# Where a fused attention and MLP kernel computes the products of its packs: beside the gates, or beside the projection

## The chip, the core and the metric

The kernel runs on one core of one Trainium2 chip. TensorE (PE) multiplies matrices into PSUM, VectorE (DVE), ScalarE (ACT) and GpSimd (POOL) do the rest, and SyncE (SP) issues the transfers. The metric is the device time of one execution, in microseconds (us). Before the change it is 1799.77 us, the median of 3 runs (1798.51 to 1803.16).

## The reference

Three stages follow each other. First an attention in which 32 packed queries per head stand between the sequence and itself, for 8 batches x 8 heads, 576 positions, 64 wide. Then a gated MLP (512 to 1536 to 512) with a root-mean-square norm, and a second MLP (512 to 2048 to 512) on 4608 tokens:

```
p_packed = softmax_attention(p, k, v)             # 32 rows per head
x        = softmax_attention(q, p_packed, p_packed)
xn = x / sqrt(mean(x*x) + 1e-6) * rms_g
g, val = xn @ w_gate, xn @ w_val
x  = (g * sigmoid(g) * val) @ w_out
h  = x @ w_in2
out = (h * sigmoid(1.702 * h)) @ w_out2
```

The weights arrive as 64-bit floats.

## The kernel before

**Two numbers for one.** Operands are fp32 values split into a high part (a cast to a reduced fp32) and a low part (the remainder), and each product is three matmuls: high x high, high x low, low x high. So most results in PSUM are read twice: ACT casts the high part, and DVE or POOL subtracts it to get the low part.

**Units, steps and pairs.** The eight batches go in four units of two batches (`o` = 0, 1). The first MLP's 1536 hidden features go in 12 steps of 128, so there are 48 steps `s`, numbered through the units. Two steps (`G = 2`) make a pair, and there are 24 pairs.

**The products of the packs.** The attention's second half is linear in `p_packed`, so the kernel never forms `x` for the gate. Per step it multiplies the packed rows (`L`, scaled by `rms_g`) with the step's columns of `w_gate` and `w_val`, and has a small matrix per head group: these are the packs' products, `prods(s)`, line 604. One call is two groups of six matmuls into a PSUM bank `ps_w` (L622), and each group is read by two ACT casts to `Wh` (L624) and two DVE subtractions to `Wl` (L625), for 64 partitions each. `Wh` and `Wl` have two buffers each.

**The gate phase.** `gateval(s, o)`, line 640, multiplies the attention weights `Aqh`, `Aql` of batch `o` with `Wh`, `Wl`: four banks `ps_g` of six matmuls (L653). ACT takes the tanh (L660), DVE makes two passes (L661, L663), which also free the banks, and when the step's `th` is complete ACT casts it to `Hh` (L668) and POOL subtracts to `Hl` (L669).

**The projection.** After both steps of a pair, `close` calls `project` for both batches and four blocks `m` of 128 output features: two banks `ps_o` of six matmuls (L684) each. A bank is added to the accumulator by DVE (L694), or copied by ACT to `add` (L698) and added by POOL (L700); in the first pair of a unit it is copied by ACT (L691).

**One pool of banks.** `ps_w`, `ps_g` and `ps_o` rotate through the same five PSUM banks (`mm`, `MMB = 5`).

**The order.** `run` is a generator: it yields the estimated ns of PE's work after each piece, and the caller puts other work in between: the attention of the next unit (its rows in the trace are `ps_at`), in unit 0 the conversion of the first MLP's weights, in unit 3 that of the second MLP's. A conversion (`convert`, line 98) is an ACT pass, four DVE passes (L106 to L109), an ACT cast (L110) and a POOL subtraction (L111). A scheduler then orders each engine's instructions by a simulated timeline, with the program's order as priority, so what stands next to what on an engine is its choice within the dependencies. Each engine runs its list in order.

**Where the products stood.** `both(s, o, ahead)` runs a gate phase and takes a group from `ahead` after its first and its fourth bank:

```
for n, ns in enumerate(gateval(s, o)):
    yield ns
    if ahead is not None and n in (0, 3):
        yield next(ahead, 0)
```

In step `s` the call for `o` = 0 gets `prods(s + 1)` (line 747). So both steps of a pair carry a product in their first half, and the projection carries none.

**The loads.** Converted weights lie in DRAM for units 1 to 3. `load_wg` (three buffers of 1 MB) and `load_wo` (two buffers of 0.5 MB) fetch them through SP's queue.

After the 48 steps the second MLP (L854, L873) runs from about 1000 us to the end; the change doesn't touch it.

Of the kernel before, what the change touches and what calls it, by code (L numbers as in the profile page):

```python
# [22 lines left out]
def fl(t):  # L23

    return t.bitcast(F32)
# [3 lines left out]
def tile_pack_attention__then__two_mlps(  # L29
# [34 lines left out]
    NF1 = F1 // P  # L64
    NF2 = F2 // P
    NM = DM // P
    G = 2
# [7 lines left out]
    WGB = 3  # L75
# [447 lines left out]
    def mlp1(cv, lp, mm, getL, getAT):  # L523
        steps = [(u, j) for u in range(NU) for j in range(NF1)]
        wo, wg, Wp, hh, Aq = {}, {}, {}, {}, {}
# [64 lines left out]
        def have(d, s):  # L590
            while s not in d:
                assert piece()

        def load_wg(s):
            if NF1 <= s < len(steps):
                wg[s] = new("wg", s)
                nc.sync.dma_start(fl(wg[s]), wg_d[steps[s][1]])

        def load_wo(s):
            if NF1 <= s:  # L600
                wo[s] = new("wo", s)
                nc.sync.dma_start(fl(wo[s]), wo_d[steps[s][1]])
# [70 lines left out]
        def project(ss, o, m):  # L673
            u, j0 = steps[ss[0]]
            b = 2 * u + o
            for e in range(2):
                cols = slice(e * HS, (e + 1) * HS)
                ps = mm.tile([P, 512], F32, tag="mm", name="ps_o")[:, :HS]
                n = 0
                for s in ss:  # L680
                    oh, ol = wo[s][:, 0], wo[s][:, 1]
                    Hh, Hl = hh[s, o]
                    for st, mv in ((oh, Hh), (oh, Hl), (ol, Hh)):
                        nc.tensor.matmul(  # L684
                            ps, st[:, m * P : (m + 1) * P], mv[:, cols], start=n == 0, stop=n == 3 * len(ss) - 1
                        )
                        n += 1
                if j0 == 0:
                    if e == 0:
                        acc[o, m] = main.tile([P, S], F32, tag=f"acc{o}{m}", name=f"acc{o}{m}", bufs=1)  # L690
                    nc.scalar.copy(acc[o, m][:, cols], ps)  # L691
                elif m == 1 or m % 2 and u:
                    a = acc[o, m][:, cols]
                    nc.vector.tensor_add(a, a, ps)  # L694
                else:
                    if e == 0:
                        t = main.tile([P, S], F32, tag="add", name="add", bufs=2)
                    nc.scalar.copy(t[:, cols], ps)  # L698
                    if e == 1:
                        nc.gpsimd.tensor_add(acc[o, m], acc[o, m], t)  # L700
                if e == 0:
                    yield 365 * G
            if j0 + len(ss) == NF1:
                nc.sync.dma_start(x2_d[b][:, m], acc[o, m])
            yield 365 * G

        def run():
            nonlocal main
            main = pools["main"]

            def close(ss):
                for s in ss:
                    have(wo, s)
                for o in range(2):
                    for m in range(NM):
                        yield from project(ss, o, m)
                for t in ss:
                    Wp.pop(t)
                    wo.pop(t)
                    used["wo"] = t + 1  # L720
                    for o in range(2):
                        hh.pop((t, o))

            def both(s, o, ahead=None):
# [4 lines that stand above are left out]
                if ahead is not None:  # L729
                    next(ahead, None)  # L730


            yield from prods(0)
            scaled(0, 0)
            yield from both(0, 0, prods(1))
            yield from both(1, 0)
            yield "attention"
            scaled(0, 1)
            yield "next"
            yield from both(0, 1)  # L740
            yield from both(1, 1, prods(2))
            yield from close([0, 1])
            for s, (u, j) in enumerate(steps):
                if s < G:
                    continue
                load_wo(s)
                yield from both(s, 0, prods(s + 1))
                load_wg(s + WGB)
                yield from both(s, 1)
                if j == NF1 - 1:  # L750
                    yield "attention"
                    scaled(u + 1, 0)
                    scaled(u + 1, 1)
                if j % G == G - 1:
                    yield from close(list(range(s - G + 1, s + 1)))
                if j == NF1 - 1:
                    yield "unit"

        return fetch, piece, run
# [152 lines left out]
    with ExitStack():  # L912
# [8 lines left out]
        with ExitStack() as st1:  # L921
# [56 lines left out]
            u, ahead = 0, None  # L978
            every = EVERY / len(todo)
            spent, done = 0.0, 0.0  # L980
            for what in run():
# [7 lines left out]
                elif what == "unit":  # L989
# [4 lines left out]
                    elif u + 1 == NU:  # L994
# [3 lines left out]
                        ahead = early()  # L998
# [60 lines left out]
```

## Time and profile before

| | |
|---|---|
| median of 3 runs | 1799.77 us |
| the profiled execution | 1803.39 us, span 1801.6 us |
| granted TensorE clock, mean | 0.985 |
| PE busy | 1714.9 us (95%), 9976 matmuls |
| DVE busy | 969.9 us (54%) |
| ACT busy | 697.0 us (39%) |
| POOL busy | 511.7 us (28%) |
| matmuls of the products, L622 | 576, from 63.6 to 977.0 us |
| matmuls of the gates, L653 | 2304, from 72.1 to 986.5 us |
| matmuls of the projection, L684 | 2304, from 112.1 to 999.2 us |

Units can be told by the transfers of finished accumulators: unit 0 ends near 363 us, unit 2 near 807 us, unit 3 near 1000 us. The page's shares are means over these stages and the second MLP, so a table of stretches is read beside it. In such a table a line gives the bounds of a stretch in us from the span's start, its length, then per engine the busy us and the number of instructions in brackets, the granted clock (1.00 is 2.4 GHz, and a stretch that lies wholly at 1.2 GHz would show 0.50), the share of the DMA engines' time and GB/s. In a list of waits a line says who waited for which instruction, for how long in total, how often, and the longest.

### The profile page before, as it was taken

How to read it: one execution, taken by the hardware profiler on the slowest of the kernel's cores; microseconds unless marked ns; L12 is line 12 of the kernel's file. 1: busy time of each engine (PE TensorE's matmuls, PEld its weight loads, DVE VectorE, ACT ScalarE, POOL GpSimd, SP SyncE). 2: the span in 40 equal slices, each digit the busy share in tenths (PEclk: the TensorE clock that was granted, in tenths of full speed). 3: DMA queues.
4: the chain of work that ended last, by engine and by line, in shares of the span. 5: the costliest groups of instructions: out<-in, count | busy, mean ns of one | idle time of the engine just before them, and what ended most of it. 6: DMA issues, size and time to landing. Idle time of an engine off the chain costs nothing.

```text
span 1801.6 us, 26222 instructions
## 1 busy us (share of the span) xinstructions
PE 1714.9 (95%) x9976; PEld 1520.3 (84%) x9976; DVE 969.9 (54%) x1971; ACT 697.0 (39%) x1644; POOL 511.7 (28%) x470
## 2 busy tenths in 40 slices
PE   7798888999999999988899999999999999999998
PEld 5587877999999999978799788888888888888887
DVE  6979999856656666688955482122222222222221
ACT  5665655665555655556544331111111111111111
POOL 2546665644554345444544230000000000000000
PEclk9989998999999999999999999999999999999999
DMA  9654445454434542268731731010101010000000
GB/s 239 187 175 148 130 142 201 148 162 134 132 115 135 161 124 94 71 205 280 261 130 43 263 94 47 1 47 1 47 1 47 1 47 17 31 1 24 1 24 24
DMA packets 154462, 186.26 MB, mean 103 GB/s; under 512 B 87648, under 2 KB 124512, under 8 KB 147296
## 3 DMA queue, kind: packets, MB, share of 16 engines
q1 hardware_dynamic: 154336, 184.58, 32.0%
q8 instruction: 79, 1.29, 0.3%
q14 instruction: 47, 0.39, 0.1%
HBM read 139.46 MB, written 45.09 MB: 102 GB/s over the span
## 4 chain that ended last, share of the span: by engine, by line
PE 78%; DVE 16%; issue 2%; DMA 2%; ACT 2%; SPq 1%; POOL 0%; ACTq 0%; DVEq 0%; POOLq 0%
PE ps_dn L873 22%; PE ps_up L854 22%; PE ps_o L684 13%; PE ps_g L653 12%; DVE w L108 3%; PE ps_w L622 3%; DVE w L109 2%; PE ps_at L264 2%; DVE Wl L625 2%; DVE w L107 2%; DVE w L106 2%; PE ps_at L253 2%; DVE th L663 1%; PE ps_at L309 1%; DVE th L661 1%
## 5 line engine op out<-in xcount | busy, mean ns | idle before, releaser
L854 PE MATMUL ps_up<-xh,wi 128*128 128x512 f32 x1152 | 381.7, 393 | 2.3 <-DMA wi<-w 1.6
L873 PE MATMUL ps_dn<-wo,gh 128*128 128x512 f32 x1152 | 356.6, 391 | 0.0
L684 PE MATMUL ps_o<-Hh,wo 128*128 128x288 f32 x1536 | 332.1, 302 | 19.3 <-DVE th L661 9.0
L860 DVE CAST gh<-gf 128x512 fp32r<-128x512 f32 x144 | 62.4, 433 | 508.1 <-ACT gf L857 508.0
L857 ACT ACTIVATE gf<-ps_up 128x512 f32<-128x512 f32 x144 | 85.9, 597 | 610.3 <-PE ps_up L854 589.6
L684 PEld LDWEIGHTS ps_o<-Hh,wo 128*128 128x128 f32 x1536 | 255.5, 191 | 24.8 <-DVE th L661 9.9
L653 PE MATMUL ps_g<-Aqh,Wh 128*128 128x288 f32 x768 | 238.9, 312 | 23.5 <-ACT Wh L624 10.0
L854 PEld LDWEIGHTS ps_up<-xh,wi 128*128 128x128 f32 x1152 | 216.2, 188 | 52.0 <-POOL wo L111 2.0
L873 PEld LDWEIGHTS ps_dn<-wo,gh 128*128 128x128 f32 x1152 | 216.3, 188 | 47.5
L653 PE MATMUL ps_g<-Aql,Wh 128*128 128x288 f32 x768 | 229.5, 299 | 0.0
L684 PE MATMUL ps_o<-Hl,wo 128*128 128x288 f32 x768 | 228.2, 299 | 0.0
L653 PE MATMUL ps_g<-Aqh,Wl 128*128 128x288 f32 x768 | 228.1, 299 | 0.0
L854 PE MATMUL ps_up<-xl,wi 128*128 128x512 f32 x576 | 225.8, 392 | 0.0
L873 PE MATMUL ps_dn<-wo,gl 128*128 128x512 f32 x576 | 224.6, 391 | 0.0
L669 POOL TENSOR_TENSOR Hl<-th,Hh 128x576 fp32r<-128x576 f32 x96 | 141.0, 1469 | 235.4 <-ACT Hh L668 228.5
L653 PEld LDWEIGHTS ps_g<-Aqh,Wh 128*128 128x128 f32 x768 | 147.8, 193 | 32.0 <-ACT Wh L624 10.6
L700 POOL TENSOR_TENSOR acc<-acc,add 128x576 f32<-128x576 f32 x90 | 133.5, 1486 | 64.9 <-ACT add L698 64.8
L625 DVE TENSOR_TENSOR Wl<-ps_w,Wh 64x512 fp32r<-64x512 f32 x192 | 131.8, 687 | 30.9 <-ACT Wh L624 27.2
L653 PEld LDWEIGHTS ps_g<-Aql,Wh 128*128 128x128 f32 x768 | 147.8, 192 | 0.0
L653 PEld LDWEIGHTS ps_g<-Aqh,Wl 128*128 128x128 f32 x768 | 146.5, 192 | 0.5 <-DVE Wl L625 0.2
L684 PEld LDWEIGHTS ps_o<-Hl,wo 128*128 128x128 f32 x768 | 146.7, 191 | 0.1
L624 ACT CAST Wh<-ps_w 64x512 fp32r<-64x512 f32 x192 | 111.2, 580 | 59.5 <-PE ps_w L622 39.8
(146 smaller groups left out, 2649.2 us busy)
## 6 DMA issues: line engine op xcount, KB each, us to landing
wg<-wg SPq DMA_DIRECT2D x48, 1024.0 KB, 5.1
wo<-wo SPq DMA_DIRECT2D x48, 512.0 KB, 4.1
x<-acc SPq DMA_DIRECT2D x32, 288.0 KB, 2.4
out_dram<-ob SPq DMA_DIRECT2D x36, 256.0 KB, 2.0
vn<-in_v_dram SPq DMA_DIRECT2D x16, 512.0 KB, 5.3
qn<-in_q_dram SPq DMA_DIRECT2D x64, 128.0 KB, 4.0
raw<-in_moe_w_in_dram SPq DMA_DIRECT2D x16, 512.0 KB, 4.1
raw<-in_moe_w_out_dram SPq DMA_DIRECT2D x16, 512.0 KB, 3.8
```

The lines of the kernel that those rows point to most:

```text
L108: nc.vector.scalar_tensor_tensor(w, top, -(1 << 30), w, op0=ALU.bitwise_and, op1=ALU.bitwise_or)
L622: nc.tensor.matmul(ps[:, a], st[:, i], mv[:, i], start=n == 0, stop=n == 2)
L624: nc.scalar.copy(Wh[rows, :, g], src)
L625: nc.vector.tensor_sub(Wl[rows, :, g], src, fl(Wh[rows, :, g]))
L653: nc.tensor.matmul(ps, st[:, o, g, c * P : (c + 1) * P], mv[:, g, cols], start=n == 0, stop=n == 3 * NG - 1)
L669: nc.gpsimd.tensor_sub(Hl, th, fl(Hh))
L684: nc.tensor.matmul(ps, st[:, m * P : (m + 1) * P], mv[:, cols], start=n == 0, stop=n == 3 * len(ss) - 1)
L700: nc.gpsimd.tensor_add(acc[o, m], acc[o, m], t)
L854: nc.tensor.matmul(ps, st[:, i], mv[:, i], start=n == 0, stop=n == 3 * NM - 1)
L857: nc.scalar.activation(gf, ps, AF.Gelu_apprx_sigmoid)
L860: nc.vector.tensor_copy(gh, gf)
L873: nc.tensor.matmul(pacc[r], st[:, r * P : (r + 1) * P], mv, start=f == 0 and n == 0, stop=f == NF2 - 1 and n == 2,)
```

## The change

The products for both steps of the next pair are computed in `close`, between the parts of the projection of the pair before: one group after the first part (`m` = 0) and one after the third (`m` = 2), for each of the two batches, which makes four groups. The gate phases carry none. The loads of `wo` for both steps of a pair are issued at its start, and `load_wg` follows each step; `Wp` entries are dropped after the step's gate phase.

```diff
--- before.py
+++ after.py
@@ -708,14 +708,18 @@
             nonlocal main
             main = pools["main"]
 
-            def close(ss):
+            def close(ss, ahead=()):
+
                 for s in ss:
                     have(wo, s)
+                rest = (ns for s in ahead for ns in prods(s))
                 for o in range(2):
                     for m in range(NM):
                         yield from project(ss, o, m)
+                        if m % 2 == 0:
+                            yield next(rest, 0)
+                yield from rest
                 for t in ss:
-                    Wp.pop(t)
                     wo.pop(t)
                     used["wo"] = t + 1
                     for o in range(2):
@@ -738,22 +742,26 @@
             scaled(0, 1)
             yield "next"
             yield from both(0, 1)
-            yield from both(1, 1, prods(2))
-            yield from close([0, 1])
-            for s, (u, j) in enumerate(steps):
-                if s < G:
-                    continue
-                load_wo(s)
-                yield from both(s, 0, prods(s + 1))
-                load_wg(s + WGB)
-                yield from both(s, 1)
-                if j == NF1 - 1:
+            yield from both(1, 1)
+            Wp.clear()
+            yield from close([0, 1], [2, 3])
+            for s in range(G, len(steps), G):
+                u, j = steps[s]
+                ss = list(range(s, s + G))
+                for t in ss:
+                    load_wo(t)
+                for t in ss:
+                    for o in range(2):
+                        yield from both(t, o)
+                    Wp.pop(t)
+                    load_wg(t + WGB)
+                last = j + G == NF1
+                if last:
                     yield "attention"
                     scaled(u + 1, 0)
                     scaled(u + 1, 1)
-                if j % G == G - 1:
-                    yield from close(list(range(s - G + 1, s + 1)))
-                if j == NF1 - 1:
+                yield from close(ss, [t + G for t in ss])
+                if last:
                     yield "unit"
 
         return fetch, piece, run
```

What the scheduler makes of it on PE, in the unit beside the second conversion. `ps_g` is a bank of the gates, `ps_w` one of the products, `ps_o` one of the projection. Before, inside a gate phase:

```order
L653 MATMUL ps_g<-Aqh,Wh 128x288
L653 MATMUL ps_g<-Aql,Wh 128x288
L653 MATMUL ps_g<-Aqh,Wl 128x288
L622 MATMUL ps_w<-wg,Lh 128x256 x2
L622 MATMUL ps_w<-wg,Ll 128x256
L622 MATMUL ps_w<-wg,Lh 128x256 x2
L622 MATMUL ps_w<-wg,Ll 128x256
L653 MATMUL ps_g<-Aqh,Wh 128x288
L653 MATMUL ps_g<-Aql,Wh 128x288
```

Now, inside a projection:

```order
L684 MATMUL ps_o<-Hl,wo 128x288
L684 MATMUL ps_o<-Hh,wo 128x288
L622 MATMUL ps_w<-wg,Lh 128x256 x2
L622 MATMUL ps_w<-wg,Ll 128x256
L622 MATMUL ps_w<-wg,Lh 128x256 x2
L622 MATMUL ps_w<-wg,Ll 128x256
L684 MATMUL ps_o<-Hh,wo 128x288
L684 MATMUL ps_o<-Hl,wo 128x288
```

The four rows of a product group (six matmuls) stood between two banks of the gates, and stand between two banks of the projection.

On DVE, in the same unit, `w` is a conversion, `th` the gate's passes, `Wl` the product's subtraction and `acc` the projection's addition. Before, inside a gate phase:

```order
L661 SCALAR_TENSOR_TENSOR th<-th,ps_g 128x288
L108 SCALAR_TENSOR_TENSOR w<-raw,w 128x512
L663 SCALAR_TENSOR_TENSOR th<-th,ps_g 128x288
L625 TENSOR_TENSOR Wl<-ps_w,Wh 64x2x256
L109 SCALAR_TENSOR_TENSOR w<-raw,w 128x512
L661 SCALAR_TENSOR_TENSOR th<-th,ps_g 128x288
L625 TENSOR_TENSOR Wl<-ps_w,Wh 64x2x256
L663 SCALAR_TENSOR_TENSOR th<-th,ps_g 128x288
L625 TENSOR_TENSOR Wl<-ps_w,Wh 64x2x256
L661 SCALAR_TENSOR_TENSOR th<-th,ps_g 128x288
L663 SCALAR_TENSOR_TENSOR th<-th,ps_g 128x288
```

Now, from the end of a gate phase into the projection:

```order
L661 SCALAR_TENSOR_TENSOR th<-th,ps_g 128x288
L663 SCALAR_TENSOR_TENSOR th<-th,ps_g 128x288
L106 TENSOR_SCALAR w<-w 128x512
L107 TENSOR_SCALAR w<-w 128x512
L108 SCALAR_TENSOR_TENSOR w<-raw,w 128x512
L106 TENSOR_SCALAR w<-w 128x512
L109 SCALAR_TENSOR_TENSOR w<-raw,w 128x512
L625 TENSOR_TENSOR Wl<-ps_w,Wh 64x2x256
L107 TENSOR_SCALAR w<-w 128x512
L694 TENSOR_TENSOR acc_10890<-acc_10890,ps_o 128x288 x2
L108 SCALAR_TENSOR_TENSOR w<-raw,w 128x512
L625 TENSOR_TENSOR Wl<-ps_w,Wh 64x2x256
```

The subtractions `Wl` stood between the gate's passes `th`, and stand between the additions `acc`; conversions lie among both.

## Rows read from the trace of the kernel before

**Rows 1.** The page: PE's totals (share, count), and its digits and DVE's.
```profile
PE 1714.9 (95%) x9976; PEld 1520.3 (84%) x9976; DVE 969.9 (54%) x1971; ACT 697.0 (39%) x1644; POOL 511.7 (28%) x470
...
PE   7798888999999999988899999999999999999998
...
DVE  6979999856656666688955482122222222222221
```

**Rows 2.** Stretches: bounds; length, busy us and count per engine, clock, DMA.
```profile
363.00:750.00 387.00, 387.00 (x2917) 376.74 (x2915) 246.96 (x558) 224.33 (x550) 175.98 (x158) 1.00 0.41 129
765.20:806.80 41.60, 34.63 (x244) 33.37 (x242) 35.05 (x59) 22.49 (x50) 19.80 (x13) 0.92 0.58 200
806.80:843.50 36.70, 31.60 (x217) 28.85 (x217) 32.32 (x51) 21.66 (x49) 16.94 (x12) 1.00 0.75 255
843.50:879.20 35.70, 31.09 (x218) 30.09 (x217) 32.13 (x55) 20.00 (x42) 19.64 (x14) 0.95 0.78 266
879.20:915.80 36.60, 30.07 (x218) 28.56 (x217) 30.31 (x53) 18.28 (x39) 16.34 (x12) 1.00 0.73 243
915.80:944.20 28.40, 28.40 (x219) 28.40 (x218) 16.00 (x32) 13.30 (x28) 11.47 (x9) 1.00 0.31 112
```

**Rows 3.** Stretches: three gate phases (one and the sum), three projections, undisturbed ones.
```profile
879.20:901.00 21.80, 16.84 (x123) 15.80 (x122) 21.41 (x38) 12.22 (x26) 8.52 (x7) 1.00 0.88 299
sum 67.50, PE 53.47 PEld 49.11 DVE 63.63 ACT 40.05 POOL 29.47; mean PE 17.82 PEld 16.37 DVE 21.21 ACT 13.35 POOL 9.82
...
sum 41.50, PE 39.30 PEld 38.39 DVE 31.14 ACT 19.89 POOL 23.45; mean PE 13.10 PEld 12.80 DVE 10.38 ACT 6.63 POOL 7.82
...
915.80:931.40 15.60, 15.60 (x122) 15.60 (x121) 11.72 (x23) 9.53 (x19) 4.55 (x4) 1.00 0.49 171
931.40:944.20 12.80, 12.80 (x99) 12.80 (x98) 4.28 (x10) 3.77 (x9) 6.92 (x6) 1.00 0.10 39
```

**Rows 4.** PE's waits, 765.2 to 915.8: us in total, times, longest.
```profile
PE ps_o L684 <- DVE th L661: 5.6, 2, 4.8
PE ps_w L622 <- DVE th L661: 5.5, 3, 2.7
```

**Rows 5.** Order of time, 857.3 to 860.8: start, us, engine, line; idle before.
```profile
...
857.77 1.93 POOL L669 TENSOR_TENSOR Hl<-th,Hh 128x576 fp32r<-128x576 f32 x1 [3.28 <-ACT Hh L668]
...
858.36 1.62 DVE L107 TENSOR_SCALAR w<-w 128x512 int32<-128x512 int32 x1
...
860.39 0.51 PE L622 MATMUL ps_w<-wg,Lh 128*128 128x256 f32 x2 [2.73 <-DVE th L661]
...
```

**Rows 6.** Stretches in unit 0, summed: four gate phases, then four projections.
```profile
...
sum 117.80, PE 98.81 PEld 90.55 DVE 111.72 ACT 76.09 POOL 65.50; mean PE 24.70 PEld 22.64 DVE 27.93 ACT 19.02 POOL 16.37
...
sum 80.30, PE 70.67 PEld 67.29 DVE 75.75 ACT 41.17 POOL 58.85; mean PE 17.67 PEld 16.82 DVE 18.94 ACT 10.29 POOL 14.71
```

**Rows 7.** Durations by line, ns: min/median/max; first and last start.
```profile
L625 DVE TENSOR_TENSOR Wl<-ps_w,Wh x192: 645/690/698, 68.5 to 979.7; 64x512 fp32r<-64x512 f32 x192
...
L624 ACT CAST Wh<-ps_w x192: 562/581/587, 64.7 to 979.1; 64x512 fp32r<-64x512 f32 x192
...
L108 DVE SCALAR_TENSOR_TENSOR w<-raw,w x104: 404/684/2502, 17.4 to 1070.3; 128x256 int32<-128x256 int32 x72, 128x512 int32<-128x512 int32 x32
```

**Rows 8.** The page: DMA issues, count, KB each, us to landing.
```profile
wg<-wg SPq DMA_DIRECT2D x48, 1024.0 KB, 5.1
```

**Rows 9.** Groups on DVE, 770 to 910: busy us, mean ns, idle before.
```profile
...
L109 DVE SCALAR_TENSOR_TENSOR w<-raw,w 128x512 int32<-128x512 int32 x20 | 20.2, 1012 | 0.1
L108 DVE SCALAR_TENSOR_TENSOR w<-raw,w 128x512 int32<-128x512 int32 x20 | 18.4, 918 | 0.4
L107 DVE TENSOR_SCALAR w<-w 128x512 int32<-128x512 int32 x20 | 17.0, 852 | 0.2
L106 DVE TENSOR_SCALAR w<-w 128x512 f32<-128x512 f32 x20 | 13.3, 664 | 7.6 <-ACT w L105 7.4
```

**Rows 10.** Waits of PE's weight loads, 363 to 750.
```profile
PEld ps_at L253 <- issue: 4.7, 28, 0.2
```

## The prediction

> **What bounds the kernel now.** I read the page first. PE is busy 95% of the span, but its digits drop to 7 and 8 in most of slices 1 to 7 and in 18 to 20, and there DVE stands at 6 to 9 [rows 1]. So there are two kinds of stretch, and the table of stretches separates them [rows 2]. From 363 to 750 us (units 1 and 2 of the attention and gate stage) PE is busy for 387.0 of 387.0 us. Nothing that only moves other engines' work can gain there. In the four pairs of steps from 765.2 to 915.8 us (all of them next to the conversion of the second MLP's weights) the pairs take 41.6, 36.7, 35.7 and 36.6 us, while the undisturbed pair behind them, 915.8 to 944.2, takes 28.4 us with as many matmuls (219 against 217 and 218). Each of the four has DVE busy for 30 to 35 us, more than PE's 28.4. These are DVE's stretches.
>
> Next I cut three of these pairs at the border between gate phase and projection [rows 3]. The three gate phases take 67.5 us and DVE is busy for 63.63 of them (94%). The three projections take 41.5 us, and DVE is busy for 31.14 (75%). The undisturbed pair gives 15.6 us for a gate phase that includes the products, and 12.8 us for a projection. So the excess over PE's own time is 67.5 - 3 x 15.6 = 20.7 us in the gate phases and 41.5 - 3 x 12.8 = 3.1 us in the projections. The time is lost where DVE has too much at once.
>
> The waits of PE say the same [rows 4]: the long ones end with L661 (the gate's first DVE pass over its bank), in front of a pack product (5.5 us in three waits) or in front of a projection (5.6 us in two). One of them in order of time [rows 5]: at 857.7 PE stops before a pack product, for 2.73 us, because no bank is free; DVE meanwhile runs a conversion pass L107 that takes 1.62 us, and the L661 that frees a bank stands behind it.
>
> The same cut in unit 0, where the first MLP's weights are converted [rows 6]: in four pairs the gate phases have DVE busy for 111.72 of 117.8 us (94.8%) and the projections for 75.75 of 80.3 us (94.3%). There DVE is full on both sides of the border.
>
> **The change part by part.** Nothing is added on PE, ACT, DVE or POOL: the products remain 576 matmuls, 192 ACT casts and 192 DVE subtractions. What moves is where they stand. Per pair of steps the gate phase loses 8 subtractions L625 of 0.69 us = 5.5 us of DVE, 8 casts L624 of 0.58 us = 4.6 us of ACT [rows 7], and 24 matmuls = 15.6 - 12.8 = 2.8 us of PE [rows 3]; the projection gets them. The product for the later step of a pair is made about half a projection earlier than before, the one for the earlier step later, but still ahead of its gate phase.
>
> *The last unit, three pairs.* DVE's need falls to 63.63 - 3 x 5.5 = 47.1 us in the gate phases and rises to 31.14 + 16.5 = 47.6 us in the projections. PE needs 3 x 12.8 = 38.4 and 3 x 15.6 = 46.8 us. DVE is the larger on both sides, so each side ends with DVE. I let DVE run at the share that it reaches today when it is the bound, 94.3%: 47.1 / 0.943 + 47.6 / 0.943 = 100.4 us, against 67.5 + 41.5 = 109.0 us. That is -8.6 us. Bounds: 0, if the pairs keep their 109 us because DVE's idle time only moves to the other side of the border; and -14 us, if DVE is never idle (47.1 + 47.6 = 94.7 us). What is late next is DVE itself.
>
> *The last unit, first pair.* It takes 41.6 us with 35.05 us of DVE [rows 2]. At 94.3% it would take 37.2 us, which is -4.4 us, but its projection also has the gate operands of the new unit to split, so that DVE has little room there. I take -2 us, between 0 and -4.4.
>
> *Unit 0.* DVE is at 94 to 95% on both sides, so moving 5.5 us from one to the other changes nothing: 0 us. Bounds: -7 us if the mix lets DVE reach 98% (187.5 us of work in 198.1 us), +3 us if its idle time grows by a third. There is one new dependency: the product of the later step wants its converted weights half a projection earlier. In the changed program's order on DVE the last conversion pass of those weights stands ahead of the first L694 of the same projection, and so ahead of the product, and I cost it at 0.
>
> *Units 1 and 2.* 0 us: PE is busy all the time and its work is the same. The cover is that the other engines keep up; DVE is busy for 247 and ACT for 224 of 387 us. What it costs if they don't is the third rival.
>
> *The DMA queue.* The scheduler issues a load when its slot comes free. The gate weights' slots now come free in the projection, two loads of 1 MB close together, and both are wanted a pair later. With 5.1 us to land [rows 8] against a pair of 28 us that is hidden: 0.
>
> Here a rule speaks against the change. The conversion passes are stretched while POOL works: L108 takes 404 ns at the least, 684 at the median and 2502 at the most, but L625, which reads PSUM, always 645 to 698 [rows 7], and the 1.62 us pass lies beside a 1.93 us POOL operation [rows 5]. The Trainium skill (SBUF — State Buffer, Who interferes with whom) says that one port pair is shared by VectorE and GpSimd as an exclusive lock, so that the loser waits for the whole instruction. The trace agrees. In the new order about one conversion per pair moves from gate phase to projection, where POOL is busy 57% of the time instead of 44% [rows 3]. By the rule such a conversion (3.4 us for its four passes [rows 9]) meets the lock 13 points more often: an estimate of +0.4 us per pair and +1 us over the unit. By the plain count it keeps its length, +0. The sum below goes without it.
>
> **The sum.** -8.6 - 2 + 0 + 0 = -10.6 us. The profiled execution took 1803.39 us (1801.6 of span and 1.8 around it), so 1792.8 us. The three timed runs have a median of 1799.77, 3.6 us below the profiled one, so I forecast 1789 us for the median of runs.
>
> **The rivals.**
> 1. *Nothing comes of it.* DVE has the same total, and its excess only follows the products across the border, as it would in unit 0, where both sides are full. For it: DVE is busy 88 to 90% over the whole of two of these pairs [rows 2], and the order is a scheduler's, whose idea of conversion times need not be the chip's. Against it: 75% in the projections. Time: no change, 1800 us.
> 2. *More comes of it.* DVE reaches 98% of these four pairs, as it does in the gate phase 879.2 to 901 (21.41 of 21.8 us): 129.8 us of DVE work [rows 2] in 132.5 us instead of 150.6, -18 us; with 97% in unit 0 another -5 us. Time: 1799.8 - 23 = 1777 us. For it: the new order alternates conversion, subtraction and accumulation one by one. Against it: DVE also waits for ACT and for raw weights, 7.4 us in the group L106 alone [rows 9].
> 3. *Slower, by the banks in units 1 and 2.* Gates, products and projections share five PSUM banks. A product's bank is held through two casts and two subtractions in turn, 0.58 + 0.69 + 0.58 + 0.69 = 2.5 us; the other four cover 4 x 0.79 = 3.2 us of projection (12.8 us / 16 each). If ACT or DVE is more than 0.6 us late, PE stops. Units 1 and 2 hold twelve pairs, eleven of them in the full stretch, with 4 such places each, 44 in all. At 0.5 us each it costs 22 us, 1789 + 22 = 1811 us; it outweighs the gain from 10.6 / 44 = 0.24 us per place on. For it: in the projections ACT also has the copies to `add`, which wait for POOL. Against it: in the gate phases the same chain stands beside tanh and two DVE passes, and PE's weight loads waited there for nothing but 0.2 us of issue at a time [rows 10].
>
> **How the numbers follow.** Forecast 0.53, rivals 0.22, 0.13 and 0.12. The forecast's own range is 1783 to 1797 (-17 to -3). About 0.3%, 5.4 us, is what a measurement of this kernel can tell from no change. Faster by more: nine tenths of the forecast, all of rival 2 and a little of rival 1, 0.62. Within 0.3%: most of rival 1, the forecast's weak end and a little of rival 3, 0.26. Slower: 0.12, nearly all of it rival 3. The range 1778 to 1801 leaves out rival 3 and the better half of rival 2, some 0.18.
>
> **What would show it.** In the changed kernel's table of stretches the pairs beside the second conversion should take 33 to 35 us instead of 36 to 37, the gate phase near 17 us and the projection too, and DVE should be near 94% on both sides. PE's waits before pack products for L661 should be gone. Unit 0's pairs should keep 45 to 56 us. Units 1 and 2 should show PE busy without a gap; gaps before L684 or L622 that end with L624, L625 or L698 are rival 3. The forecast is wrong if the four pairs keep their 150 us, or if unit 0 moves by more than 7 us.

## The result, and the profile after

The changed kernel takes 1779.85 us (median of 4 runs, 1779.39 to 1780.74), the kernel before beside it 1801.47 (1798.51 to 1803.37). The ratio is 0.9882, 95% interval 0.9865 to 0.9899: faster by 21.6 us, where the forecast had 10.6. The profiled executions have spans of 1801.6 and 1779.0 us, 22.6 apart, and all that follows divides these 22.6.

PE's totals and digits and DVE's digits in the page after, against [rows 1]:

```profile
PE 1711.8 (96%) x9976; PEld 1516.7 (85%) x9976; DVE 958.3 (54%) x1971; ACT 693.8 (39%) x1644; POOL 509.2 (29%) x470
...
PE   7889888999999999999899999999999999999998
...
DVE  5889999756667566688964572222222222222221
```

PE's digits show where, but are coarse: beside the second conversion slices 18 and 19 rise from 8 to 9, and of slices 2 to 7, beside the first, two rise and one falls. The instruction counts are the same, but two busy times are not: PE's fell by 3.1 us and DVE's by 11.6 us. A "busy" time of DVE is thus no fixed amount of work; we come back to that.

To compare stretches, I cut both executions at three gate matmuls L653: the first of all, the first of unit 1, and the first of unit 2's last pair, where the second conversion begins. What follows that are the last seven pairs, one of unit 2 and six of unit 3; the prediction calls them the last unit, and its "first pair" is unit 2's last. The cut is not quite fair. In the new order one step's product (12 matmuls, half of the 15.6 - 12.8 = 2.8 us of [rows 3], so 1.4 us) is made before each border instead of behind it, so the new unit 0 has 1.4 us more work and the new last seven pairs 1.4 us less. And 16 matmuls of the next unit's attention (`ps_at`) are done in unit 0 now: the eleven pairs have 636 of them instead of 652. PE has no gap in these pairs, so the 1.8 us that they lose are this moved work. The last column corrects for both.

| us | before | after | difference | with equal work |
|---|---|---|---|---|
| first gate matmul at | 72.1 | 75.9 | +3.8 | +3.8 |
| unit 0 | 291.0 | 279.2 | -11.7 | -15.0 |
| eleven pairs of units 1 and 2 | 402.2 | 400.3 | -1.8 | 0 |
| last seven pairs | 234.3 | 221.4 | -12.9 | -11.5 |
| rest | 802.1 | 802.2 | +0.1 | +0.1 |

The first line is not the change's: up to the first gate PE, DVE, ACT and POOL run the same instructions in the same order in both kernels. The kernels below with a full conversion keep that order too, and their first gate starts at 72.3 to 75.4 us; what moves it stays open. Taken with it, unit 0 ends 8.0 us earlier, 11.2 us with equal work. So the last seven pairs give about the sum that was forecast for them, and unit 0 gives 11 to 15 us that were forecast as nothing.

The stretches after, against [rows 2]: the eleven pairs of units 1 and 2, the first five of the last seven pairs, and at the end the four full pairs of unit 0.

```profile
355.09:755.42 400.33, 400.33 (x3014) 390.13 (x3013) 251.79 (x568) 224.72 (x556) 184.78 (x168) 1.00 0.39 124
755.42:789.83 34.41, 32.05 (x243) 31.43 (x242) 27.60 (x55) 20.76 (x49) 18.38 (x13) 1.00 0.65 233
789.83:821.06 31.23, 29.81 (x218) 28.58 (x217) 28.44 (x49) 20.13 (x44) 13.80 (x10) 1.00 0.69 236
821.06:854.35 33.29, 30.26 (x219) 28.63 (x217) 29.75 (x53) 20.67 (x43) 18.50 (x13) 1.00 0.77 277
854.35:891.26 36.91, 31.37 (x219) 30.03 (x218) 35.59 (x55) 18.85 (x39) 20.31 (x15) 0.95 0.67 246
891.26:922.87 31.61, 29.64 (x218) 28.52 (x217) 21.36 (x43) 15.39 (x33) 11.85 (x9) 1.00 0.49 173
135.24:319.31 184.07, 165.20 (x1136) 152.76 (x1134) 181.30 (x388) 115.82 (x317) 122.61 (x120) 0.96 0.55 170
```

And the same four pairs of unit 0 in the kernel before, whose two sides are in [rows 6]:

```profile
128.86:327.05 198.19, 169.57 (x1147) 157.93 (x1146) 187.56 (x390) 117.35 (x317) 124.39 (x123) 0.94 0.49 152
```

Unit 0: DVE is busy 181.30 of 184.07 us (98.5%) where it was busy 187.56 of 198.19 (94.6%). Both parts moved, its idle time (10.6 to 2.8 us) and the time its work takes (6.3 us less for 388 instead of 390 instructions). The length of these four pairs is not quite comparable: 12 matmuls of the attention have gone to the pair before them, so the unit as a whole, in the table above, is the better measure of the gain.

The border between gate phase and projection after: the sums of the second to fourth of the last seven pairs, gate phases first, against [rows 3], then of the four pairs of unit 0 against [rows 6].

```profile
sum 44.02, PE 41.43 PEld 39.95 DVE 40.07 ACT 25.15 POOL 22.70; mean PE 13.81 PEld 13.32 DVE 13.36 ACT 8.38 POOL 7.57
```
```profile
sum 57.41, PE 50.01 PEld 47.28 DVE 53.71 ACT 34.51 POOL 29.92; mean PE 16.67 PEld 15.76 DVE 17.90 ACT 11.50 POOL 9.97
```
```profile
sum 84.65, PE 77.16 PEld 71.52 DVE 83.72 ACT 50.63 POOL 56.90; mean PE 19.29 PEld 17.88 DVE 20.93 ACT 12.66 POOL 14.23
```
```profile
sum 99.42, PE 88.04 PEld 81.23 DVE 97.58 ACT 65.19 POOL 65.71; mean PE 22.01 PEld 20.31 DVE 24.39 ACT 16.30 POOL 16.43
```

The three pairs take 101.4 us (forecast 100.4, before 109.0), with 93.8 us of DVE (forecast 94.7). But more than the products crossed the border: gate phases have 40.1 us of DVE instead of the forecast 47.1, projections 53.7 instead of 47.6. The scheduler moved conversion passes with the products: the gate phases have 24 of them where they had 44, the projections 42 where they had 19.

PE's waits in 755.4 to 891.3 us after, against [rows 4]:

```profile
PE ps_w L622 <- DVE acc L694: 4.9, 3, 2.3
PE ps_g L653 <- DVE acc L694: 2.1, 1, 2.1
PE ps_o L684 <- DVE Wl L625: 1.6, 1, 1.6
```

The waits for the gate's pass L661 in front of a product or a projection are gone. A product now waits for the projection's addition L694, for about as long in all.

### The profile page after: what moved, and what is told of

It reads as the page before. It is cut to its first block, busy times and chain, and to the rows that moved or that the text cites. A ratio compares the mean times of both kernels' runs of the same rounds, so it can differ in the third digit from the quotient of the medians.

```text
span 1779.0 us, 26239 instructions
## 1 busy us (share of the span) xinstructions
PE 1711.8 (96%) x9976; PEld 1516.7 (85%) x9976; DVE 958.3 (54%) x1971; ACT 693.8 (39%) x1644; POOL 509.2 (29%) x470
## 4 chain that ended last, share of the span: by engine, by line
PE 78%; DVE 14%; issue 3%; DMA 2%; ACT 2%; POOL 0%; SPq 0%; ACTq 0%; DVEq 0%; POOLq 0%
PE ps_dn L881 22%; PE ps_up L862 22%; PE ps_g L653 12%; PE ps_o L684 12%; PE ps_w L622 3%; PE ps_at L264 2%; DVE w L108 2%; DVE w L109 2%; DVE w L106 2%; PE ps_at L253 2%; DVE Wl L625 2%; DVE w L107 1%; PE ps_at L309 1%; PE ps_at L386 1%; DVE th L661 1%
## 5 line engine op out<-in xcount | busy, mean ns | idle before, releaser
L684 PE MATMUL ps_o<-Hh,wo 128*128 128x288 f32 x1536 | 347.8, 302 | 10.7 <-DVE Wl L625 4.1
L653 PE MATMUL ps_g<-Aqh,Wh 128*128 128x288 f32 x768 | 236.5, 309 | 15.7 <-ACT Wh L624 9.8
L653 PE MATMUL ps_g<-Aql,Wh 128*128 128x288 f32 x768 | 229.1, 299 | 0.0
L653 PE MATMUL ps_g<-Aqh,Wl 128*128 128x288 f32 x768 | 227.7, 298 | 0.0
L653 PEld LDWEIGHTS ps_g<-Aqh,Wh 128*128 128x128 f32 x768 | 147.2, 192 | 22.4 <-ACT Wh L624 10.5
L625 DVE TENSOR_TENSOR Wl<-ps_w,Wh 64x512 fp32r<-64x512 f32 x192 | 131.9, 687 | 57.3 <-ACT Wh L624 53.9
L653 PEld LDWEIGHTS ps_g<-Aql,Wh 128*128 128x128 f32 x768 | 147.1, 192 | 0.1
L653 PEld LDWEIGHTS ps_g<-Aqh,Wl 128*128 128x128 f32 x768 | 146.2, 191 | 0.0
```

Source lines behind the costliest of these rows:

```text
L625: nc.vector.tensor_sub(Wl[rows, :, g], src, fl(Wh[rows, :, g]))
L653: nc.tensor.matmul(ps, st[:, o, g, c * P : (c + 1) * P], mv[:, g, cols], start=n == 0, stop=n == 3 * NG - 1)
L684: nc.tensor.matmul(ps, st[:, m * P : (m + 1) * P], mv[:, cols], start=n == 0, stop=n == 3 * len(ss) - 1)
```

## The experiments

The spans of all kernels, cut at the same three gate matmuls (us, profiled executions, not corrected for moved work):

| | ratio to before, 95% | first gate | unit 0 | eleven pairs | last seven |
|---|---|---|---|---|---|
| before | 1 | 72.1 | 291.0 | 402.2 | 234.3 |
| changed | 0.9882 (0.9865 to 0.9899) | 75.9 | 279.2 | 400.3 | 221.4 |
| loads only | 1.0001 (0.9992 to 1.0009) | 72.3 | 291.0 | 402.2 | 233.9 |
| unit 0 only | 0.9924 (0.9910 to 0.9938) | 73.0 | 276.4 | 401.6 | 234.0 |
| last unit only | 0.9963 (0.9949 to 0.9978) | 72.5 | 287.4 | 402.2 | 227.5 |
| units 1, 2 only | 0.9967 (0.9954 to 0.9979) | 72.4 | 293.4 | 400.4 | 226.8 |
| spread in the gates | 1.0041 (1.0025 to 1.0057) | 73.6 | 297.0 | 401.4 | 234.6 |
| bunched in the projection | 0.9903 (0.9888 to 0.9919) | 73.8 | 284.2 | 401.8 | 222.8 |
| light, before | 0.9692 (0.9673 to 0.9712) | 69.1 | 261.4 | 400.4 | 212.7 |
| light, changed | 0.9630 (0.9611 to 0.9650) | 69.1 | 257.2 | 399.3 | 206.1 |
| additions off DVE | 0.9965 (0.9952 to 0.9978) | 73.4 | 292.1 | 399.3 | 229.3 |
| additions on DVE | 0.9853 (0.9836 to 0.9869) | 73.2 | 282.2 | 399.2 | 219.0 |
| low part on DVE | 0.9824 (0.9806 to 0.9842) | 75.4 | 282.6 | 399.7 | 212.7 |
| the same, last unit only | 0.9813 (0.9800 to 0.9826) | 74.0 | 279.9 | 400.3 | 212.8 |

**The loads alone.** The kernel before, with the new places of `load_wo` and `load_wg`:

```diff
-                load_wo(s)
+                if s % G == 0:
+                    for t in range(s, s + G):
+                        load_wo(t)
                 yield from both(s, 0, prods(s + 1))
-                load_wg(s + WGB)
                 yield from both(s, 1)
+                load_wg(s + WGB)
```

> The products stay in the gate phases; only the loads are issued as in the changed kernel (both load_wo of a pair at its start, load_wg after each whole step). Theory: the gain comes from where the products stand, so this kernel keeps the time before, 1801 us within 3 us, and the four pairs of the last unit keep 41.6, 36.7, 35.7 and 36.6 us. Rival: the loads' new places make the gain (the weights come earlier or collide less with the raw weights of the conversion); then this kernel takes about 1780 us.

1802.43 us, ratio 1.0001. The loads do nothing, and the rival falls.

**One part of the units at a time.** The changed kernel, with the products beside the projection for the steps of some units and in the gate phases for the others (`late(t)` is `prods(t)` or nothing):

```diff
+            beside = lambda t: t < len(steps) and steps[t][0] in (0,)   # or (3,), or (1, 2)
...
-                    for o in range(2):
-                        yield from both(t, o)
+                    yield from both(t, 0, late(t + 1))
+                    yield from both(t, 1)
...
-                yield from close(ss, [t + G for t in ss])
+                yield from close(ss, [t + G for t in ss if beside(t + G)])
```

> The products stand beside the projection for the steps of unit 0 alone; the steps of units 1 to 3 have them in the gate phases as before. Theory (DVE, full in unit 0, is kept busy 98% instead of 94.6% of the time by the new order): 8 to 12 us less than before, 1789 to 1793 us, with the four pairs of unit 0 near 184 us instead of 198. Rival (the prediction's step: nothing moves in unit 0, and what the changed kernel is ahead there is a chance of its order that it loses again): less than 3 us of change, 1799 to 1802 us.

> The products stand beside the projection for the steps of the last unit alone. Theory (the prediction's 10.6 us, DVE's overfull gate phases beside the second conversion): 9 to 13 us less than before, 1788 to 1792 us, and unit 0 takes what it took. Rival (the gain of the last unit only comes because unit 0 has got ahead and its weights and attention are ready earlier): less than 4 us of change.

> The products stand beside the projection for the steps of units 1 and 2 alone. Theory: PE is busy without a gap in these units whatever the order, so 0 to 2 us less than before, 1799 to 1802 us. With unit 0 alone and the last unit alone the three should add up to the 21.6 us of the whole change. Rival (the parts depend on each other): the three together give less than 15 us, and the rest needs all three.

Unit 0 alone: 1788.03 us against 1803.25, and 0.76% of it is 13.7 us. That is unit 0's own gain, and the step that forecast 0 is wrong. The last unit alone: 1795.17 us, 6.7 us by the ratio, less than expected. In its profile unit 0 was 3.6 us shorter too, though its four engines ran the same instructions in the same order there as in the kernel before, so that is how much unit 0 can scatter from one execution to another. Units 1 and 2 alone: 1796.75 us, 6.0 us, where at most 2 were expected. Their eleven full pairs are 1.7 us shorter, but 12 of their attention matmuls have gone to unit 0, which is 2.4 us longer. The gain lies in the pair behind these, which is unit 2's last: I had counted it with the last unit. In the kernel before, and with units 1 and 2 alone:

```profile
765.24:806.77 41.53, 34.56 (x244) 33.30 (x242) 35.02 (x59) 22.46 (x50) 19.76 (x13) 0.92 0.58 200
```
```profile
766.24:799.89 33.65, 31.18 (x232) 30.06 (x230) 27.70 (x53) 18.76 (x45) 16.61 (x12) 1.00 0.58 206
```

One of the two products of its gate phases has gone to the projection before it (12 matmuls less), and it is 7.9 us shorter. With the last unit alone it is shorter too, 38.1 us with 12 matmuls more, and in the changed kernel, with as many as before, 34.4. The three kernels together give 26.4 us, 5 more than the whole, which is about what the intervals of the four ratios leave open; this pair is where two of them gain the same thing. In the kernel before it holds one long stop; the rows are the stop and the 8.7 us behind it:

```profile
784.20:788.97 4.77, 0.00 (x1) 0.01 (x1) 4.77 (x9) 2.25 (x6) 1.41 (x1) 0.73 0.33 137
788.97:797.67 8.70, 8.53 (x48) 8.30 (x48) 8.61 (x14) 3.73 (x9) 5.96 (x4) 0.76 0.36 111
```

PE stands 4.77 us while DVE catches up. The granted clock is 0.73 in the stop and 0.76 in the 8.7 us behind it, so part of both is at the lower level, and the 48 matmuls there take 8.53 us, where the 96 of a whole undisturbed projection take 12.80 us [rows 3] and half of them 6.4: 2.1 us more. A long stop is paid for a second time.

**Spread within the gate phases.** The kernel before, with one product group in the gate phase of each batch instead of both in the first:

```diff
+                ahead = prods(s + 1)
-                yield from both(s, 0, prods(s + 1))
+                yield from both(s, 0, ahead, (1,))
-                yield from both(s, 1)
+                yield from both(s, 1, ahead, (1,))
...
-                    if ahead is not None and n in (0, 3):
+                    if ahead is not None and n in at:
```

> The products stay in the gate phases, but are spread: one group of the next step's product in the gate phase of each batch, instead of both in the first. Theory (what counts is the border: the gate phase has more DVE work than PE work, and the projection has room for it): little, 0 to 4 us less than before, 1797 to 1801 us, since each pair's gate phases keep 63.6 us of DVE work for three of them. Rival (what counts is the bunching, two groups within one short gate phase, and any even spread would do): 10 to 20 us less, 1781 to 1791 us.

1809.38 us, ratio 1.0041: 7.5 us slower. Both were off, the rival by far. The last seven pairs stay as they were (234.6), though not one by one: the first takes 33.65 us, and the fourth, which holds stops of 3.5 and 2.5 us now, 42.89. Spread within the gate phases in this way the products gain nothing; what gained had crossed the border.

**Bunched in the projection.** The changed kernel, with its four groups behind the first four parts of the projection:

```diff
-                        if m % 2 == 0:
+                        if o == 0:
                             yield next(rest, 0)
```

> The changed kernel, with its four product groups one after each of the first four parts of the projection (all within the first batch), instead of after every second part. Theory (what counts is the border: the products leave the gate phases, where DVE has too much): nearly the whole gain stays, 1779 to 1785 us. Rival (what counts is that the products are spread evenly): a good part of the gain goes, 1788 us or more, with waits of PE for the product's subtraction in the first half of the projections.

1786.51 us, ratio 0.9903: 17.5 of 21 us stay, between the two expectations. In the profiles the last seven pairs keep all but 1.4 us of their gain; unit 0 loses 5.0 of its 11.7. So in the last pairs the border counts, and in unit 0, by one execution, the spread counts as well.

**A lighter conversion.** Two of its four DVE passes are left out, in the kernel before and in the changed one:

```diff
-        nc.vector.scalar_tensor_tensor(w, top, -(1 << 30), w, op0=ALU.bitwise_and, op1=ALU.bitwise_or)
-        nc.vector.scalar_tensor_tensor(w, low, 29, w, op0=ALU.logical_shift_right, op1=ALU.bitwise_or)
```

> The kernel before with two of the four DVE passes of a conversion left out (the third and fourth, which bring in sign and low bits of a weight, so that part of the computation is missing). About 5 us of DVE work per large conversion goes, in unit 0 and in the last unit. Theory (DVE is what these stretches wait for): 25 to 45 us less than before, 1756 to 1776 us. Rival (the stretches wait for the raw weights or for ACT): less than 10 us.

> The changed kernel with the same two conversion passes left out (the same part of the computation is missing). Theory (the change gains because DVE has too much at once where the products stood): with DVE relieved the change has little left to gain, so this kernel is 0 to 8 us below the light version of the kernel before, not 21 us. Rival (the change gains in another way, through PE's banks or the loads, for which DVE's load does not matter): it stays 17 to 22 us below it.

1746.48 and 1735.51 us. With that much less on DVE the kernel before loses 55 us, more than expected: these stretches do wait for DVE. The change still gains 11.0 us, half of what it gained, between the expectations. The four full pairs of unit 0, light, before and changed:

```profile
118.49:296.38 177.89, 163.66 (x1162) 154.94 (x1161) 140.28 (x304) 118.94 (x323) 122.03 (x126) 0.96 0.58 179
```
```profile
122.15:291.51 169.36, 160.04 (x1151) 151.19 (x1149) 139.14 (x303) 117.18 (x319) 120.26 (x121) 0.98 0.61 186
```

DVE is busy 79% of the first, and the change still takes 8.5 us from it. Part of that is work that has moved to the pair before (12 attention matmuls fewer); unit 0 as a whole is 4.2 us shorter, some 7 us with equal work, where the full conversion gave 15. PE's waits that end with an instruction of DVE fall in it from 17.2 to 10.9 us (with the full conversion from 27.1 to 19.6). So a DVE that is busy 95% of the time is not needed for a gain, and "DVE is full" is at most half of the cause. I put the rest down to moments at which several works want DVE at once; no run isolates them, and the light kernels also have only half of the passes that the next experiment is about.

**The additions off DVE, and on it.** In the first and the last unit, the projection's additions all by ACT and POOL, or all by DVE:

```diff
-                elif m == 1 or m % 2 and u:
+                elif m % 2 and 0 < u < NU - 1:                    # off DVE
+                elif m == 1 or m % 2 and u or u in (0, NU - 1):   # on DVE
```

> The changed kernel, and in the first and the last unit the projection's additions that DVE made go through an ACT copy and a POOL addition like the others. Per pair of the last unit 8 additions of about 0.8 us leave DVE. Theory (DVE is the wall in both stretches, 98% busy in unit 0): 4 to 10 us less than the changed kernel, 1770 to 1776 us. Rival (POOL's additions hold up DVE's conversion passes, and the two add buffers hold up PE): as the changed kernel or slower, 1780 to 1790 us.

> The changed kernel, with the projection's additions of the first and the last unit all made by DVE, none by ACT and POOL: the reverse of the run that took them off DVE. In the trace of the changed kernel 29 additions L700 stand on POOL in unit 0 and 17 between 755 and 923 us; as 92 passes of DVE of 0.44 us they add 40 us to it. Plain count (a pass costs what it costs): 25 to 40 us slower, 1805 to 1820 us. Theory of the port (DVE's conversion passes are stretched by 0.6 us for each us that they lie beside a POOL operation, and 22.4 and 11.9 us of them lie beside L700): 21 us of the 40 come back, so 10 to 20 us slower, 1790 to 1800 us.

Off DVE: 1795.83 us, 16 us slower than the changed kernel; the rival had the sign and still too small a loss. Both of its reasons show: the conversion passes below, and PE's waits for the copies to `add` (L698), 6.7 us in unit 0 where the changed kernel has 0.8, and 9.3 us in the first five of the last seven pairs instead of 0.7. On DVE: 1776.73 us. Its interval overlaps that of the changed kernel, so it is not clearly faster, but the plain count is refuted by over 20 us, and even the theory of the port was too dark. Unit 0 is 3.0 us longer and the last seven pairs 2.4 us shorter. Why the 59 additions that came to DVE in unit 0 cost so little is seen in its conversion passes. The rows are line, tile, count, busy us, mean ns and idle time before; first the kernel before, then the changed one, then with the additions on DVE:

```profile
L108 DVE SCALAR_TENSOR_TENSOR w<-raw,w 128x256 int32<-128x256 int32 x58 | 45.8, 792 | 0.3
L109 DVE SCALAR_TENSOR_TENSOR w<-raw,w 128x256 int32<-128x256 int32 x59 | 43.8, 745 | 0.4
L107 DVE TENSOR_SCALAR w<-w 128x256 int32<-128x256 int32 x58 | 29.1, 504 | 0.4
L106 DVE TENSOR_SCALAR w<-w 128x256 f32<-128x256 f32 x58 | 26.5, 461 | 2.5 <-ACT w L105 2.4
```
```profile
L109 DVE SCALAR_TENSOR_TENSOR w<-raw,w 128x256 int32<-128x256 int32 x58 | 38.2, 659 | 0.1
L108 DVE SCALAR_TENSOR_TENSOR w<-raw,w 128x256 int32<-128x256 int32 x58 | 37.1, 639 | 0.3
L107 DVE TENSOR_SCALAR w<-w 128x256 int32<-128x256 int32 x58 | 32.4, 558 | 0.3
L106 DVE TENSOR_SCALAR w<-w 128x256 f32<-128x256 f32 x58 | 30.9, 533 | 0.1
```
```profile
L108 DVE SCALAR_TENSOR_TENSOR w<-raw,w 128x256 int32<-128x256 int32 x58 | 36.9, 639 | 0.2
L109 DVE SCALAR_TENSOR_TENSOR w<-raw,w 128x256 int32<-128x256 int32 x59 | 31.1, 528 | 0.1
L106 DVE TENSOR_SCALAR w<-w 128x256 f32<-128x256 f32 x58 | 31.0, 534 | 0.1
L107 DVE TENSOR_SCALAR w<-w 128x256 int32<-128x256 int32 x58 | 23.8, 412 | 0.1
```

The same passes take 145.2 us, 138.6 and 122.8. With the additions off DVE it is 145.9. A second execution of the first two orders (last unit only; low part on DVE in the last unit alone) gives 143.4 and 139.1. What stretches the passes is seen one by one in the changed kernel's order of time (start, us, engine, line):

```profile
202.47 0.41 DVE L109 SCALAR_TENSOR_TENSOR w<-raw,w 128x256 int32<-128x256 int32 x1
...
202.93 1.58 POOL L669 TENSOR_TENSOR Hl<-th,Hh 128x576 fp32r<-128x576 f32 x1 [1.43 <-ACT Hh L668]
...
203.40 1.38 DVE L109 SCALAR_TENSOR_TENSOR w<-raw,w 128x256 int32<-128x256 int32 x1
```

The first L109 has no POOL operation beside it and takes 0.41 us; the second begins in the middle of one and takes 1.38. It is so throughout: of the 116 passes L108 and L109 in unit 0 of the changed kernel, 62 overlap no operation of POOL, and none of these took less than 0.37 or more than 0.43 us; the 54 others took up to 2.30 us, 0.92 on average. At the lengths without overlap (0.28 us for L106 and L107, 0.41 for L108 and L109) the unit's 58 conversions would take 80 us instead of 138.6, an estimate from these rows.

**The low part on DVE.** The subtraction to `Hl`, in the first and the last unit:

```diff
-            nc.gpsimd.tensor_sub(Hl, th, fl(Hh))
+            (nc.gpsimd if 0 < u < NU - 1 else nc.vector).tensor_sub(Hl, th, fl(Hh))
```

> The changed kernel, with the subtraction to Hl in the first and the last unit made by DVE instead of POOL. In the trace of the changed kernel POOL has 24 of them in unit 0 (1.54 us each) and 20 between 755 and 923 us (1.50 us). On DVE one should take 0.77 us by its columns and the 0.68 us of L625, 34 us in all. Plain count: 20 to 34 us slower, 1800 to 1814 us. Theory of the port (23.7 and 10.2 us of conversion passes lie beside L669 and are stretched by about 0.6 us per us): 21 us come back, 8 to 15 us slower, 1788 to 1795 us; and the mean of a conversion's four passes in unit 0 falls from 2.39 us to about 2.1.

1771.36 us, ratio 0.9824: 8.5 us below the changed kernel, where both expected it slower. In unit 0 the four conversion lines sum to 124.6 us, 2.15 us per conversion, as the theory of the port had it, and DVE's new subtractions more than take it back:

```profile
L669 DVE TENSOR_TENSOR Hl<-th,Hh 128x576 fp32r<-128x576 f32 x24 | 21.2, 884 | 0.0
```

Unit 0 is no shorter (282.6 against 279.2). In the last unit DVE takes them almost for nothing. The five pairs that hold all 80 passes of the second conversion, in the changed kernel and with the low part on DVE:

```profile
755.42:922.87 167.45, 153.14 (x1107) 147.19 (x1106) 142.74 (x251) 95.81 (x206) 82.84 (x57) 0.99 0.66 234
757.71:916.43 158.72, 150.51 (x1107) 145.64 (x1106) 143.50 (x267) 95.91 (x206) 63.28 (x41) 1.00 0.69 247
```

16 subtractions (12.6 us) have come to DVE, the 80 passes have fallen from 65.9 to 57.1 us, and DVE is busy 0.8 us longer. The 8.7 us come from its idle time, 24.7 us and now 15.2: the same work stands closer together, and PE's waits that end with an instruction of DVE fall from 11.6 to 6.1 us. What shortened the idle time, the shorter passes or an earlier `Hl`, is not shown; no wait of PE ended with POOL's `Hl` in either kernel.

**The same in the last unit alone.** `nc.vector if u == NU - 1 else nc.gpsimd` in that line:

> The changed kernel, with the subtraction to Hl made by DVE in the last unit alone; unit 0 keeps it on POOL. With DVE making it in both units, unit 0 ended 2.9 us later than in the changed kernel (358.0 against 355.1 us) and the last unit took 212.7 instead of 221.4 us. Theory (the last unit's gain is its own, and unit 0 pays for nothing): unit 0 as in the changed kernel, 212 to 215 us for the last unit, 1768 to 1773 us. Rival (the order of one unit shifts the other, and what the two units gave and lost was chance): 1774 us or more, no better than the changed kernel by 0.3%.

1769.33 us, ratio 0.9813 (0.9800 to 0.9826): the lowest of all, though its interval overlaps the one just before; 33.9 us below the kernel before and 10.5 below the changed one, whose interval it does not touch. The unit's gain is its own: 212.8 us for the last seven pairs, and 279.9 in unit 0, where the order is the changed kernel's.

## Why the prediction was right in its sign and half its size

The time lies within the stated range of 1778 to 1801 us, but outside the forecast's own 1783 to 1797, and one of the prediction's signs of being wrong came: unit 0 moved by more than 7 us.

**The bound was read rightly.** PE's lost time lay beside the two conversions, and a move that adds no work gained there. The gain went with the products (loads only: 1.0001), and with their crossing of the border (spread in the gates: 1.0041).

**The last seven pairs, -10.6 us, came out at -11.5, with the parts wrong.** The three pairs took 101.4 us for a forecast of 100.4. But 3.3 of these 7.7 us come back in the fifth pair, 31.6 us instead of 28.3, with 43 DVE instructions instead of 32: conversions were put off to it, which the sum did not have. And the first pair gave 7.1 us where the bounds ended at 4.4. They were taken from DVE's share alone, and left out that the stop of 4.77 us also lowers the granted clock behind it. So the three pairs gave 4.4 us net where 8.6 were forecast, and the first pair 7.1 where 2 were; that the sum fits is luck.

**Unit 0, 0 us, is the step that failed:** "DVE is at 94 to 95% on both sides, so moving 5.5 us from one to the other changes nothing". Unit 0 alone gives 13.7 us. Two assumptions stand in that sentence. One is that 94% is as full as DVE gets; it reached 98.5%. The other is that DVE's 187.5 us were work; 145 of the 262 us that it is busy in the whole unit are conversion passes that lie partly beside POOL, and the new order cut them by 6.6 us (4 to 7 over two executions of each order). My lower bound, 7 us "if the mix lets DVE reach 98%", held the second fixed. The light kernels suggest that the two are not all of it: with DVE busy 79% the change still took some 7 us of equal work from the unit. That this comes from fewer moments in which gate, product and conversion ask for DVE together is argued, not shown.

**The rule on the port was used with the wrong sign.** The Trainium skill (SBUF — State Buffer, Who interferes with whom) has VectorE and GpSimd share a port pair as an exclusive lock. The rows agree: 0.41 us against 1.38 for the same pass, while passes that read PSUM keep their time (L625, [rows 7]). But I worked out from POOL's mean share on either side of the border that the conversions would pay 1 us more, which I left out of the sum. (The row of L108 that I read the stretch from also mixes passes of 256 and 512 columns, 0.41 and 0.68 us without overlap, so its median says little.) They got 6.6 us cheaper in unit 0, and 3.0 us cheaper beside the second conversion (80 passes, 68.9 us [rows 9] and now 65.9). Which pass lies beside which POOL operation is decided by the order, one by one, and a mean share doesn't tell it.

**Units 1 and 2, 0 us:** right. Their eleven pairs took 1.8 us less, with PE busy without a gap before and after, and that is the 16 attention matmuls that the new order had done in unit 0. The third rival, PSUM banks, falls: PE did not wait there.

**The DMA queue, 0:** right, as the kernel with the loads alone shows.

**The rivals.** The second, 1777 us, has the nearest time and half its mechanism: DVE rose to 98%, but in unit 0, for which it had 5 us. In the four pairs for which it had 18, DVE reached 121.4 / 135.8 = 89%. The first, nothing gained, falls.

**What stays open:** how unit 0's gain divides between less idle DVE, shorter passes and granted clock, since they depend on each other; what moves the first gate by up to 3.8 us; and how far chance in the scheduler's order decides which pair of the last seven holds a long stop, which moved single pairs by 6 to 8 us.

## What to carry to other kernels

A secondary engine's 94% is no ceiling and its busy time no constant: before a move is priced at zero because "it is full on both sides", ask how much of that time is waiting for a shared port, and bound the gain with both the idle time and the stretch. When one engine's passes wait for another's accesses, count the work of the two together: an operation of 12.6 us in all, taken from the idler one and given to the busy one, cost the busy one 0.8 us here, and the stretch became shorter. Price a stall with its aftermath, since a stop of some 5 us also lowered the granted clock behind it.

## What the runs showed of the hardware

An operation moved from POOL to DVE cost DVE much less than its own length. Beside the second conversion 16 subtractions of two SBUF tiles (12.6 us) came to DVE and its busy time rose by 0.8 us, since the conversion's 80 passes fell from 65.9 to 57.1 us. In unit 0 24 of them (21.2 us) raised it by 4.2 us (257.5 to 261.6), and 59 additions that read PSUM (26.1 us) by 5.7 us (to 263.2). The other way round, ten more additions on POOL and twenty fewer passes on DVE left DVE no less busy in unit 0 (259.3 against 257.5 us), and the unit 12.9 us longer; PE's waits for the copies to `add` rose there by 5.9 us, so not all of that is DVE's. These three units hold 5 or 6 attention matmuls more than the changed kernel's, so differences of 1 us among them say nothing.

A conversion pass of DVE between SBUF tiles was never long without an operation of POOL beside it (the 62 of 256 columns above, L108 and L109, stayed within 0.37 to 0.43 us, and others took up to 2.30 us beside one), while L625, which reads PSUM, kept 0.65 to 0.70 us with POOL beside it and without.
